# Windowed attention and an MLP-mixer in one kernel: the last batch's normalising in two tasks, one key copy on another engine, new ranks

## The chip, the cores and the metric

The kernel runs on one core of a Trainium2 chip. Inputs arrive in float32, the arithmetic on the matrix engine is in bfloat16, and the result is float32. The metric is the device time of one execution in microseconds. The engines are called by the names of the profile: PE is TensorE (matrix products), PEld its weight loads, DVE is VectorE, ACT is ScalarE, POOL is GpSimd and SP is SyncE, which issues DMAs.

## The reference

Four batches of eight heads, sequence 768, head size 64. Each query sees the 128 newest keys and the first four keys (the "sinks"). The eight heads' outputs side by side are the input x (768 x 512) of a mixer layer with a token product and a channel product.

```python
scores = (q @ k.T) / sqrt(64)              # per batch and head, 768 x 768
keep = (pos_k < 4) | ((pos_q - pos_k >= 0) & (pos_q - pos_k < 128))
a = exp(where(keep, scores, -1e9) - max)   # then a / sum(a)
x = concat_heads(a @ v)                    # 4 x 768 x 512
h = relu(x.T @ w_tok1) @ w_tok2            # 512 x 768
u = x + h.T
out = u + relu(u @ w_ch1) @ w_ch2          # w_ch1 512 x 1536, w_ch2 1536 x 512
```

## The kernel before

**The work.** The 32 pairs of batch and head are cut into eight groups of four heads, numbered g = 0 to 7; batch b holds the groups 2b and 2b + 1. Inside a group, j = 0 and 1 are its two pairs of heads. The rows of a group's key axis are six tiles of 128.

For each group the steps are, in the order of the data: load q and k in float32; cast to bfloat16 (`make_cast`); transpose on PE into a PSUM bank and copy the result to SBUF as `qT` and `kT` (`make_turn`; groups 5 to 7 transpose by DMA instead); copy eight sink columns of `kT` into `ks` (`make_ks`); score products on PE, where for groups 0 and 1 a product with `mneg` first puts the mask into PSUM, and `exp` on ACT into `pT` (`make_scores`); for groups 2 to 7 the mask is applied to `pT` afterwards by POOL or DVE; the product with v, six row tiles a group (`make_pv`). v carries a column of ones, so that each of the four heads has 64 sums and, as the 65th, its denominator. Normalising is a reciprocal of four denominators per row (`nc.vector.reciprocal`, 128 x 4) and a multiplication of 128 x 256 from PSUM into `x_b`.

After the two groups of a batch come the token products (`make_tok`) and the channel products (`make_channel`). Batches 1 to 3 make the second channel product from seven half-size products per pair of row tiles, with sums that DVE forms (`products`), and batch 3 some of the first too (`pairs_of_tiles`).

**The order.** No loop sets the order of the instructions. Every step is a `Task` with the engines that may run it, an estimated cost on each, the tasks it depends on, and a priority. `Plan.order` runs a list schedule over these: whenever an engine is free by the estimates, it takes the ready task of lowest priority number whose PSUM bank is free. A task that may run on several engines is taken by one only if it would end there no more than 0.12 us after the best. The instructions are then emitted in that planned order, so each engine runs its own fixed list, and real waits are semaphores. The priorities are overwritten from `RANK`, one number for each of 963 tasks in the order in which they are made.

**What the change touches.** `FIRST_TURNS` (line 19) names, for the four pairs of heads of groups 0 and 1, the engine of the PSUM-to-SBUF copy of q and of k. `SPLIT_TC` cuts these copies of group 0 into two halves of 384 columns. The entry of the second pair of heads reads `[('ACT', 'DVE'), 'ACT']`: its q copies may run on ACT or DVE, its two k copies run on ACT (line 439 in the profile, where a copy on DVE or POOL is line 441). `KS_ENG` (line 48) names the engines of the sink-column copies. In `make_pv`, groups 0 and 1 (`g < GB`, GB is 2) normalise in two tasks: the reciprocal on DVE (line 969) and the multiplication, on DVE (line 975) or, for group 1, also on ACT, where it would be four ACTIVATE instructions of 64 columns with the reciprocal as a per-row scale (line 978). Groups 2 to 7 have one task on DVE with both instructions (lines 962 and 963). For b of 2 or 3 this task also waits for the earlier readers of `x_b`, the list `old`.

Other names in the rows: `ps_sa`, `ps_sb` are the two double PSUM banks of the scores, `ps_ga` to `ps_gd` the four single banks; `rca` to `rcd` hold reciprocals; `vsink` is the sinks' part of v, made by DVE from `vs_b`; L1070 and L1068 are the relu on DVE and ACT, L1233 and L1143 the sums of the fast products, L1291 and its neighbours the reads of their results, and L484 issues loads.

Of the kernel before, what the change touches and what calls it, by code (L numbers as in the profile page):

```python
# [18 lines left out]
FIRST_TURNS = [[('ACT', 'DVE'), 'ACT'], [('ACT', 'DVE'), 'ACT'], ['DVE', 'DVE'], ['DVE', 'ACT']]  # L19
# [28 lines left out]
KS_ENG = {0: ('POOL', 'ACT', 'DVE'), 1: ('POOL', 'ACT', 'DVE'), 2: ('POOL',), 3: ('ACT',), 4: ('POOL', 'ACT', 'DVE'), 5: ('ACT', 'DVE'),  # L48
    6: ('ACT', 'DVE'), 7: ('ACT', 'DVE')}
# [7 lines left out]
RANK = [-500, 24, 27, 449, 556, 90, 80, 0, 0, 50, 50, 150, 100, 200, 150, 1557, 74, 556, 219, 901, 901, 1065, 1145, 1361, 1701, 2045,  # L57
    1972, 2310, 2575, 2855, 3040, -150, 210, 350, 300, 330, 1773, 1470, 1468, 1409, 1411, 1823, 3185, 3282, 100, 259, 239, 205, 529,
    441, 514, 701, 663, 12, 531, 585, 585, 803, 857, 904, 570, 625, 662, 836, 1004, 1070, 1212, 1232, 978, 783, 604, 682, 873, 890,
    1001, 1017, 1122, 1134, 1252, 1269, 1449, 1440, 1631, 1634, 1820, 1607, 1622, 1746, 1916, 1972, 2056, 2011, 2069, 2414, 2134, 2278,  # L60
    2211, 2076, 2192, 2225, 981, 1023, 1075, 1303, -80, 1101, 1155, 1359, 1497, 1218, 1243, 1456, 1658, 1757, 1741, 1402, 927, 1673,
    1786, 1330, 1627, 1802, 1987, 1822, 1997, 1906, 2226, 2157, 2089, 2268, 2285, 2171, 2215, 2218, 2278, 2338, 1814, 2488, 2447, 2471,
    2243, 2478, 2531, 2269, 2618, 2348, 2413, 2500, 2313, 2399, 2479, 2522, 2566, 2598, 2630, 2650, 3144, 2587, 2619, 2651, 2972, 3042,
    3021, 3102, 2824, 2894, 2923, 2683, 2775, 2825, 3070, 3151, 2874, 2924, 3720, 3190, 3624, 4010, 3559, 3645, 3364, 3450, 3169, 3360,
    4114, 4200, 3429, 3485, 3764, 3550, 3349, 3317, 3234, 3323, 3886, 3972, 3396, 3782, 4049, 4135, 4340, 4179, 4179, 4835, 4121, 3907,
    3984, 4070, 4405, 4508, 4320, 4556, 4657, 4846, 4722, 4889, 4592, 4682, 4940, 5048, 5243, 5329, 5308, 5394, 4787, 4965, 5380, 5489,
    5864, 5609, 5816, 6220, 6350, 6424, 6396, 6544, 6734, 6764, 6582, 6949, 7169, 7560, 7620, 7684, 7166, 7635, 7851, 7980, 8234, 8166,
    8276, 8556, 8685, 8750, 3803, 3379, 3879, 3250, 3951, 4009, 4307, 4313, 3662, 3717, 3629, 3747, 3921, 3905, 4244, 4328, 4418, 4535,
    4613, 4719, 5103, 5204, 5230, 5320, 4854, 5140, 4982, 4860, 5217, 5353, 4942, 5124, 5488, 5569, 5574, 5630, 5695, 5751, 5730, 5801,
    5765, 5851, 4780, 4997, 4738, 5070, 4877, 4961, 4843, 4898, 5313, 5300, 5346, 5361, 5516, 5536, 5542, 5595, 5686, 5800, 5924, 5993,  # L70
    5947, 6087, 6234, 5724, 5712, 5815, 6260, 7238, 6150, 6622, 6717, 6815, 6630, 7305, 6683, 6899, 6975, 7172, 7010, 7242, 7044, 7222,
    6008, 6035, 5283, 5969, 7257, 7374, 7252, 7428, 7592, 7694, 7859, 7548, 7634, 7734, 7721, 7808, 7984, 7764, 7867, 8129, 7971, 8042,
    8284, 7807, 7927, 8409, 3698, 4250, 4385, 4595, 4547, 4690, 4642, 4812, 9086, 8872, 8664, 8690, 8791, 8967, 9202, 9332, 8981, 9067,
    8916, 9004, 9157, 9223, 9332, 9418, 9267, 9369, 9866, 9972, 9625, 9711, 9560, 9706, 9610, 9776, 10427, 10513, 10232, 10318, 10167,
    10253, 10362, 10448, 10535, 10621, 10640, 10686, 10665, 10751, 10730, 10816, 10926, 11012, 10766, 11132, 10834, 11220, 10425, 10536,
    10678, 10788, 10740, 10835, 11039, 11720, 11205, 11274, 11355, 11480, 10297, 10383, 10795, 10883, 11417, 11528, 11548, 11634, 11613,
    11274, 11402, 11700, 11744, 11831, 11878, 11774, 10861, 10947, 10991, 11087, 11482, 11569, 12203, 12289, 11679, 12006, 12093, 12337,
    12398, 12485, 12532, 12411, 11205, 11322, 11810, 11896, 11875, 11962, 11941, 12027, 12072, 12911, 12997, 13614, 12107, 12224, 12271,
    12519, 5174, 4939, 5189, 5299, 5339, 5993, 5851, 5776, 5971, 6218, 6074, 6098, 6299, 6363, 6156, 6291, 6332, 6197, 6517, 6237, 6182,
    6915, 6565, 7443, 7491, 7560, 6838, 6967, 6993, 6898, 6900, 7014, 7606, 7773, 7637, 7275, 7959, 7992, 8253, 8302, 8014, 8102, 8084,  # L80
    8452, 8049, 8252, 8118, 8202, 5654, 5389, 5484, 5579, 5769, 5934, 5999, 6104, 7160, 6664, 6586, 6935, 7423, 6752, 7481, 8186, 8206,
    8363, 8446, 8536, 8729, 8747, 8816, 9046, 9237, 9146, 9263, 8583, 8643, 8779, 9007, 9270, 9349, 9125, 9158, 9397, 8842, 9421, 8892,
    9456, 9542, 9585, 9652, 9510, 9722, 8425, 7911, 7890, 8018, 9095, 9181, 9160, 9847, 9994, 10075, 10299, 9951, 10015, 10174, 10492,
    10556, 10564, 10037, 10135, 10519, 10080, 10194, 10769, 10124, 10254, 11249, 12716, 12802, 12271, 12357, 12544, 12550, 12529, 12615,
    12594, 12680, 12846, 12952, 12781, 12867, 13055, 13141, 13120, 13206, 13202, 13268, 13267, 13353, 13390, 13476, 13455, 13541, 13625,
    13711, 13965, 14051, 14200, 13986, 14030, 14116, 14205, 14327, 14490, 14576, 14903, 14989, 14360, 14446, 14783, 14849, 14968, 15054,
    15754, 15240, 14145, 14193, 14280, 14598, 14782, 15042, 15340, 15286, 15838, 15083, 15164, 15245, 14270, 14374, 14425, 14511, 15653,
    15739, 15544, 15630, 16404, 15294, 15512, 15902, 15979, 16065, 16298, 16248, 14555, 14646, 14632, 14729, 15913, 16171, 16130, 16228,
    16221, 16523, 16610, 16057, 16589, 16717, 16781, 16731, 14698, 14829, 15219, 15431, 16196, 16302, 16327, 16413, 16458, 16372, 16779,
    16544, 16654, 16750, 16831, 16618, 9034, 9129, 9224, 9414, 9649, 9604, 9699, 9984, 8297, 9726, 10044, 10347, 10981, 10894, 11119,  # L90
    12276, 12276, 12456, 12539, 12630, 12659, 12827, 12737, 13016, 13167, 13076, 13193, 12526, 12719, 12965, 12853, 13183, 12719, 13185,
    13253, 13332, 13377, 13356, 13417, 13520, 13576, 13545, 13546, 13590, 13676, 9949, 9794, 9319, 10424, 10079, 11024, 11374, 11469,
    9581, 10883, 11402, 12006, 12775, 11564, 12713, 13648, 13628, 13691, 13790, 13880, 13971, 14105, 14226, 14253, 14343, 14433, 13897,
    14009, 14247, 14485, 14646, 14829, 14621, 14699, 14828, 14873, 14852, 15223, 15033, 15090, 15068, 15140, 15107, 15333, 13835, 13921,
    13769, 13871, 15398, 15484, 15478, 15565, 15761, 16142, 15998, 15718, 15782, 15873, 15609, 15674, 15748, 15870, 15961, 16123, 16034,
    16108, 16348, 16087, 16168, 16473, 14326, 13779, 13832, 14241, 17053, 17124, 17195, 17266, 16720, 16806, 16785, 16871, 16850, 16936,
    16915, 17001, 16980, 17066, 17110, 17190, 17240, 17323, 17142, 17272, 17326, 17402, 17456, 17549, 17610, 17532, 17662, 17595, 17656,
    17735, 17795, 17045, 17153, 17175, 17261, 17305, 17091, 17370, 17428, 17435, 17502, 17467, 17500, 17553, 17865, 17872, 17781, 17842,
    17760, 17857, 17827, 17888, 17925, 17973, 17597, 17688, 17675, 17781, 17792, 17878, 17890, 17976, 18217, 18303, 18432, 18368, 18356,
    18442, 18421, 18507, 18077, 17525, 18200, 18316, 18496, 18621, 18702, 18723, 17971, 18029, 18173, 18268, 17955, 18363, 18020, 18430,  # L100
    18748, 18837, 18683, 18770, 18945, 18617, 18803, 19031, 18476, 19162, 19210, 19105, 18086, 18396, 18151, 18463, 18814, 18900, 18889,
    18966, 19141, 19010, 19097, 19228, 19338, 19425, 19473, 19302, 18526, 18609, 18552, 18689, 19207, 19293, 19272, 19359, 19403, 18737,
    19392, 19469, 19555, 19614, 17123, 19490, 19564, 19684, 19589, 19664, 19528, 19622, 19657]
STRASSEN = {1, 2, 3}
EARLY_P = {1: 0, 2: 0, 3: 4}
TURNS = '10 20 11 21 60 50 61 40 70 51 41 30 12 71 22 62 52 31 72 32 42'
S_CHUNK = 2
S_ENG = {1: ('DVE',), 2: ('DVE',), 3: ('DVE',)}
T_ENG = ('POOL', 'DVE')
HALF_PAIRS = 2  # L110
TILES = '05 0b 04 0a 03 p0 09 02 08 p1 15 1b 14 1a 13 19 12 18'

SEM = 0.05
# [214 lines left out]
def dve(n):  # L328
    return n * 0.00104 + 0.065
# [11 lines left out]
def kernel(  # L341
# [14 lines left out]
    B, H, S, D = q.shape  # L356
# [1161 lines left out]
```

## Time and profile before

| what | value |
|---|---|
| time, median of 13 runs | 199.39 us (198.97 to 200.59) |
| the profiled execution's own time | 200.41 us |
| its span, first to last instruction | 198.7 us |
| instructions | 4652 |
| granted TensorE clock | 1.00 throughout |
| DMA | 31.01 MB, mean 156 GB/s |

The profiled execution took 200.41 us, of which 1.7 us lie outside its span; it is 1.02 us above the median. A row of the windows view names a stretch and then the busy time of each engine in it, with the number of instructions in brackets. A row of the timeline gives start, duration, engine, source line, operation, tiles written and read, shapes, and, in square brackets, the idle time before it and what ended it. A PE row's duration contains the time in which the array waited in mid-instruction, so a PE that is busy for a whole stretch can still have lost time there.

### The profile page before, as it was taken

Reading aid. Unit: us, or ns where it says so; the run is one execution under the profiler, and the core shown is the slowest. Engines: PE = TensorE matmul, PEld = TensorE weight load, DVE = VectorE, ACT = ScalarE, POOL = GpSimd, SP = SyncE. Lnnn points to the kernel's source line nnn. Section 1 sums busy time; section 2 is a strip of 40 time slices with the busy share of each in tenths; the row PEclk is TensorE's granted clock in tenths of the full one; section 3 lists DMA queues with packets and bytes.
Section 4 is the critical chain, followed back from the end, with each engine's and each line's share of the span. In section 5 each row is a group of like instructions: output and inputs, shape, how many; then the busy total and the mean of one; then the engine's idle time right before and its main releaser. Section 6 shows DMA issues by size and latency. Waiting matters only on the chain.

```text
span 198.7 us, 4652 instructions
## 1 busy us (share of the span) xinstructions
PE 191.8 (97%) x1795; PEld 129.5 (65%) x1795; DVE 140.1 (71%) x321; ACT 107.3 (54%) x189; POOL 86.7 (44%) x151
## 2 busy tenths in 40 slices
PE   7899999999998999999999999999999999999993
PEld 2443876656675564665765787667687787567882
DVE  3688871587759677835558776367898979189973
ACT  2799378889898644177535301966843002765100
POOL 8984432125999763078770110891990000120000
PEclk9999999999999999999999999999999999999999
DMA  5999999999399979699999996250000157200044
GB/s 175 367 221 181 208 206 332 229 259 213 84 273 185 269 158 154 180 139 214 235 187 117 185 204 210 110 137 0 0 3 0 30 131 240 80 3 0 26 158 136
DMA packets 75016, 31.01 MB, mean 156 GB/s; under 512 B 63666, under 2 KB 71474, under 8 KB 74994
## 3 DMA queue, kind: packets, MB, share of 16 engines
q1 hardware_dynamic: 44082, 18.85, 42.4%
q0 software_dynamic: 29680, 10.22, 42.4%
q10 hardware_dynamic: 1232, 1.64, 2.3%
q8 instruction: 14, 0.23, 0.5%
q14 instruction: 8, 0.07, 0.1%
HBM read 26.77 MB, written 6.29 MB: 166 GB/s over the span
## 4 chain that ended last, share of the span: by engine, by line
PE 85%; ACT 4%; DVE 3%; DMA 3%; POOL 2%; issue 1%; POOLq 0%; DVEq 0%
PE ps_gd L1111 8%; PE ps_gb L1111 8%; PE ps_ga L1111 7%; PE ps_gd L1258 6%; PE ps_gb L1258 5%; PE ps_gc L1111 5%; PE ps_gc L1258 4%; PE ps_ga L1258 3%; DMA q32a<-in_q_dram 3%; PE ps_sa L1258 2%; PE ps_gb L1366 2%; PE ps_sa L830 2%; PE ps_sb L830 2%; PE ps_gd L1366 2%; PE ps_gd L1009 2%; PE ps_ga L1366 1%
## 5 line engine op out<-in xcount | busy, mean ns | idle before, releaser
L1111 PEld LDWEIGHTS <-w_ch 128*128 128x128 bf16 x352 | 33.3, 98 | 20.5 <-issue 0.6
L1258 PEld LDWEIGHTS <-v 128*128 128x128 bf16 x222 | 21.2, 98 | 4.2 <-issue 0.2
L1068 ACT ACTIVATE v<-ps_gb 128x384 bf16<-128x384 f32 x20 | 9.8, 490 | 17.9 <-PE ps_gb L1111 13.6
L1068 ACT ACTIVATE v<-ps_gc 128x384 bf16<-128x384 f32 x13 | 6.4, 489 | 16.2 <-PE ps_gc L1111 15.5
L1111 PE MATMUL ps_gd<-uTa,w_ch 128*128 128x384 bf16 x72 | 14.7, 326 | 0.0
L1068 ACT ACTIVATE v<-ps_gd 128x384 bf16<-128x384 f32 x19 | 9.3, 491 | 6.4 <-PE ps_gd L1111 6.2
L1068 ACT ACTIVATE v<-ps_ga 128x384 bf16<-128x384 f32 x16 | 7.8, 490 | 5.4 <-PE ps_ga L1111 5.3
L1366 PEld LDWEIGHTS <-v 128*128 128x128 bf16 x72 | 6.3, 97 | 6.8 <-issue 1.3
L1111 PE MATMUL ps_gb<-uTa,w_ch 128*128 128x384 bf16 x52 | 10.6, 326 | 0.0
L1009 PEld LDWEIGHTS <-w_tok 128*128 128x128 bf16 x96 | 9.2, 98 | 1.8 <-issue 0.2
L1111 PE MATMUL ps_gb<-uTb,w_ch 128*128 128x384 bf16 x48 | 9.8, 326 | 0.0
L441 POOL CAST of<-u_sbb 128x256 f32<-128x256 bf16 x1 | 0.7, 691 | 19.6 <-DVE vab L1143 19.6
L484 POOL DMA_DIRECT2D vaa<-in_v_dram x4 | 6.0, 1492 | 7.3 <-PE ps_gc L943 6.0
L1111 PE MATMUL ps_ga<-uTa,w_ch 128*128 128x384 bf16 x40 | 8.1, 326 | 0.0
L1111 PE MATMUL ps_ga<-uTb,w_ch 128*128 128x384 bf16 x40 | 8.1, 326 | 0.0
L484 POOL DMA_DIRECT2D vab<-in_v_dram x4 | 5.8, 1452 | 5.3 <-PE ps_gb L1033 2.4
L885 POOL TENSOR_TENSOR pTa<-pTa,mask 128x512 bf16<-128x512 bf16 x2 | 2.3, 1153 | 13.1 <-ACT pTa L874 13.1
L874 ACT ACTIVATE pTc<-ps_sb 128x768 bf16<-128x768 f32 (+1 forms) x6 | 5.5, 924 | 3.6 <-PE ps_sb L830 3.6
L441 DVE CAST kba<-k32a 128x768 bf16<-128x768 f32 x4 | 4.1, 1046 | 4.6 <-DMA k32a<-in_k_dram 4.6
L441 POOL CAST qbb<-q32b 128x768 bf16<-128x768 f32 x5 | 4.1, 820 | 7.1 <-DMA q32b<-in_q_dram 7.1
L441 POOL CAST kbb<-k32b 128x768 bf16<-128x768 f32 x5 | 4.5, 893 | 5.8 <-DMA k32b<-in_k_dram 5.8
L830 PEld LDWEIGHTS <-kTa 64*128 64x128 bf16 x96 | 3.5, 94 | 4.8 <-issue 3.8
(453 smaller groups left out, 593.9 us busy)
## 6 DMA issues: line engine op xcount, KB each, us to landing
q32a<-in_q_dram SPq DMA_DIRECT2D x4, 384.0 KB, 4.6
vaa<-in_v_dram POOLq DMA_DIRECT2D x4, 384.0 KB, 11.2
vab<-in_v_dram POOLq DMA_DIRECT2D x4, 384.0 KB, 11.3
w_ch<-in_moe_w_ch_dram POOLq DMA_DIRECT2D x3, 512.0 KB, 15.2
w_ch<-in_moe_w_ch_dram POOLq DMA_DIRECT2D x2, 768.0 KB, 19.8
q32b<-in_q_dram SPq DMA_DIRECT2D x8, 192.0 KB, 4.6
k32b<-in_k_dram SPq DMA_DIRECT2D x8, 192.0 KB, 5.7
out_dram<-oa SPq DMA_DIRECT2D x4, 256.0 KB, 7.0
```

What stands on the lines that cost most here:

```text
L441: on(t).tensor_copy(out=o, in_=i)
L484: t = add(eng, hold, lambda t: e.dma_start(out=o, in_=i), deps, prio=prio, dma=work, run=run)
L830: nc.tensor.matmul(half(slot, i)[:, at:at + w].rearrange("p (c q) -> p c q", q=P), qkT(kT, g, j)[ds(64 * i, 64), kt], qkT(qT, g, j)[ds(64 ...
L874: nc.scalar.activation(dst[:, :, 512 * u:512 * u + w], ps_s[slot.at[1]][:, :, 0:w], AF.Exp, scale=scale)
L885: on(t).tensor_tensor(out=dst[:, :, 0:2 * P], in0=dst[:, :, 0:2 * P], in1=mask0.rearrange("p i c q -> p i (c q)"), op=ALU.mult)
L1009: nc.tensor.matmul(flat(slot)[:, 0:GH * D], w_tok1[:, n, ts(tt, P)], x[:, n, ds(a * GH * D, GH * D)], start=(n == 0), stop=(n == NT - 1))
L1068: nc.scalar.activation(o, i, AF.Relu)
L1111: nc.tensor.matmul(flat(slot)[:, 0:HS], w_ch1[:, c, ts(ft, P)], uT_[:, c, ds(half * HS, HS)], start=(c == 0), stop=(c == NC - 1))
L1258: nc.tensor.matmul(flat(slot)[:, 0:cw], A[n][0][:, x, ts(i, P)], W[n][:, x, ds(c0, cw)], start=(first and x == 0), stop=(x == NH - 1), ski ...
L1366: nc.tensor.matmul(flat(slot)[:, 0:cw], v1[:, ft, ts(st, P)], w_ch2[:, ft, ds(c0, cw)], start=(ft == 0), stop=(ft == NF - 1 and (b > 0 or ...
```

## The change

Three switches and the table of ranks. The second pair of heads' key copy in group 0 goes to DVE. The sink-column copies may run on other sets of engines in four groups. The groups 6 and 7, which are the last batch, normalise in two tasks as the groups 0 and 1 do, so that their multiplication may run on DVE or ACT; it keeps the wait for `old`, the reciprocal does not have it. As each of 12 tasks becomes two, `RANK` has 975 entries instead of 963. Of the older entries 211 change by more than 15, up to 1200, and 18 by 15 or less; the rest keep their value.

```diff
-FIRST_TURNS = [[('ACT', 'DVE'), 'ACT'], [('ACT', 'DVE'), 'ACT'], ['DVE', 'DVE'], ['DVE', 'ACT']]
+FIRST_TURNS = [[('ACT', 'DVE'), 'ACT'], [('ACT', 'DVE'), 'DVE'], ['DVE', 'DVE'], ['DVE', 'ACT']]
...
-KS_ENG = {0: ('POOL', 'ACT', 'DVE'), 1: ('POOL', 'ACT', 'DVE'), 2: ('POOL',), 3: ('ACT',), 4: ('POOL', 'ACT', 'DVE'), 5: ('ACT', 'DVE'),
-    6: ('ACT', 'DVE'), 7: ('ACT', 'DVE')}
+KS_ENG = {0: ('ACT', 'DVE'), 1: ('POOL', 'ACT', 'DVE'), 2: ('POOL', 'ACT', 'DVE'), 3: ('ACT', 'DVE'), 4: ('POOL', 'ACT', 'DVE'), 5:
+    ('ACT', 'DVE'), 6: ('ACT', 'DVE'), 7: ('ACT', 'DVE')}
...
-RANK = [-500, 24, 27, 449, 556, 90, 80, 0, 0, 50, 50, 150, 100, 200, 150, 1557, 74, 556, 219, 901, 901, 1065, 1145, 1361, 1701, 2045,
...
+RANK = [-500, 24, 37, 449, 556, 90, 80, 0, 0, 50, 50, 150, 100, 200, 150, 1517, 74, 556, 219, 901, 901, 1065, 1145, 1361, 1701, 2045,
...
+NORM_ACT = {6, 7}
...
-            if g < GB:
+            old = [*mixers[b - 2].add, *mixers[b - 2].tok1, *mixers[b - 2].s_use[2]] if b >= 2 else []
+            if g < GB or g in NORM_ACT:
                 def er(t, slot=slot, r=r):
                     nc.vector.reciprocal(r, flat(slot)[:, 0:GH * D1].rearrange("p (h d) -> p h d", h=GH)[:, :, D:D1])
...
                 m = add("DVE", 0.1, er, [m, last_rc], prio=pr(g, "no"))
-                G.norm.append(add(("ACT", "DVE") if g else "DVE", {"ACT": 0.8, "DVE": dve(GH * D)}, e, [m], prio=pr(g, "no"),
+                G.norm.append(add(("ACT", "DVE") if g else "DVE", {"ACT": 0.8, "DVE": dve(GH * D)}, e, [m, *old], prio=pr(g, "no"),
                                   slot=slot, frees=True))
                 rc_use[slot_rc] = G.norm[-1]
                 continue
-            old = [*mixers[b - 2].add, *mixers[b - 2].tok1, *mixers[b - 2].s_use[2]] if b >= 2 else []
             G.norm.append(add("DVE", dve(4) + dve(256) + 0.1, e, [m, *old, last_rc], prio=pr(g, "no"), slot=slot, frees=True))
```

Ranks that the prediction speaks of, by the task they belong to (before, then after; unchanged where one number stands):

| task | rank |
|---|---|
| group 0, second pair: q copies, two halves | 857, 904 |
| group 0, second pair: k copies, two halves | 1004, 1070 |
| group 1, first pair: cast of q, cast of k | 981 to 1011, 1023 to 1053 |
| group 0: sink-column copies | 1212; 1232 to 592 |
| group 0: v product of row tiles 1 and 2 | 1607 to 1307, 1916 to 1316 |
| group 1, row tile 0: v product | 2089 to 2699 |
| group 4, first pair: exp of the first and second of its units | 6915 to 6695, 6565 to 6535 |
| group 6: normalising of six row tiles | 13253 ... 13676 to pairs 12885, 12909 ... 13338, 13383 |
| group 7: normalising of six row tiles | 14699 ... 15333 to pairs 15084, 15265 ... 15487, 15532 |

## The prediction

> **What bounds the kernel now.** I read the page first, then the windows of 5 us, then the PE's own waits, and last the timelines of ACT and DVE in the stretches where PE loses time.
>
> ```profile
> PE 191.8 (97%) x1795; PEld 129.5 (65%) x1795; DVE 140.1 (71%) x321; ACT 107.3 (54%) x189; POOL 86.7 (44%) x151
> ```
>
> PE is busy for 97% of the span, and in the channel products it is at its pace: groups of four matmuls of 384 columns start every 0.65 us in the chain of waits, 163 ns each. So a change that leaves the products alone can only win back what PE loses to waits. The PE waits view names, in 8 to 24 us and in 56 to 66 us:
>
> ```profile
> PE ps_sb L813 <- ACT pTc L874: 0.4, 1, 0.4
> PE ps_sa L817 <- ACT pTa L874: 0.2, 1, 0.2
> ...
> PE ps_gb L837 <- DVE h1b L1070: 0.4, 1, 0.4
> PE ps_ga L1366 <- DVE kTa L441: 0.4, 1, 0.4
> PE ps_gb L751 <- DVE kba L441: 0.2, 1, 0.2
> ```
>
> That is 0.6 us of waits for `exp` in front and 1.0 us for DVE in the middle. A busy PE hides more. From the starts of its rows less the columns at the pace above, and less the 0.09 us that every change between score products and full-height products costs, I get 1.3 us in 8 to 24 us (0.18 at 8.2, 0.23 at 10.0, 0.18 at 16.9, 0.43 at 18.0, 0.24 at 21.8), 1.4 us in 60 to 64.3, and 0.3 us in 146 to 152. The start (0.6 us for the first cast) and the last 3.3 us (reads and stores after PE's end at 195.4) aren't touched by a switch.
>
> In front the bound is ACT, with DVE close behind. The windows of 8:15, 15:22, 58:65 and 150:156:
>
> ```profile
> 8.00:15.00 7.00, 6.74 (x77) 3.50 (x73) 5.32 (x9) 6.95 (x13) 6.34 (x9) 1.00 1.62 255
> 15.00:22.00 7.00, 6.51 (x90) 3.29 (x87) 5.50 (x16) 6.53 (x9) 3.28 (x7) 1.00 1.73 189
> 58.00:65.00 7.00, 6.08 (x63) 4.16 (x61) 5.71 (x7) 5.68 (x9) 6.91 (x12) 1.00 1.67 221
> 150.00:156.00 6.00, 6.00 (x68) 4.89 (x67) 5.58 (x16) 2.03 (x5) 0.00 (x0) 1.00 0.00 0
> ```
>
> ACT has 6.95 of 7 us (fourth busy figure), DVE 5.32. The timelines of the two engines there:
>
> ```profile
> 10.17 0.53 ACT L439 ACTIVATE kTa<-ps_gd 128x384 bf16<-128x384 bf16 x1
> 10.54 0.86 ACT L874 ACTIVATE pTa<-ps_sb 128x768 bf16<-128x768 f32 x1
> 11.23 0.55 ACT L439 ACTIVATE kTa<-ps_gd 128x384 bf16<-128x384 bf16 x1
> 11.60 1.10 ACT L874 ACTIVATE pTb<-ps_sa 128x1024 bf16<-128x1024 f32 x1
> 14.83 0.83 ACT L874 ACTIVATE pTc<-ps_sb 128x768 bf16<-128x768 f32 x1
> ...
> 9.30 1.02 DVE L441 COPY qTa<-ps_gc 128x384 bf16<-128x384 bf16 x2 [1.07 <-PE ps_gc L751]
> 10.24 0.55 DVE L441 CAST qbb<-q32b 128x768 bf16<-128x768 f32 x1
> 10.70 0.74 DVE L441 CAST kbb<-k32b 128x768 bf16<-128x768 f32 x1
> 12.96 0.96 DVE L441 COPY kTb<-ps_ga 128x768 bf16<-128x768 bf16 x1 [0.24 <-PE ps_ga L751]
> ```
>
> The reader should see that the two key copies stand between `exp` instructions on ACT, and that the moved copies would stand on DVE in front of the casts from which the next group's scores come.
>
> For the normalising, DVE's timelines at 151 and at 23.6 us:
>
> ```profile
> 151.36 0.17 DVE L962 RECIPROCAL rcc<-ps_gb 128x4 f32<-128x4 f32 x1
> 151.56 0.42 DVE L963 TENSOR_TENSOR x_bb<-ps_gb,rcc 128x256 bf16<-128x256 f32 x1
> 151.91 0.17 DVE L962 RECIPROCAL rcd<-ps_gd 128x4 f32<-128x4 f32 x1
> ...
> 23.62 0.17 DVE L969 RECIPROCAL rcc<-ps_ga 128x4 f32<-128x4 f32 x1
> 23.71 0.15 DVE L969 RECIPROCAL rcd<-ps_gc 128x4 f32<-128x4 f32 x1
> ```
>
> In one task each multiplication starts 0.20 us after its reciprocal and a pair takes 0.55 us. In two tasks the reciprocals overlap, 0.09 us apart.
>
> **What the Trainium skill says.** "ScalarE: Activation LUTs", section "What ACT_TABLE_LOAD costs", prices an ACTIVATE at 186 ns + 0.833 ns a column, 93 ns more for each per-row operand, and lets neighbours overlap by 93 ns. 384 columns give 506 ns; the trace has 486 to 552, so it agrees. "TensorE: Matmul & The Clock Gate", section "Back-to-back issue gap", has N / 2.4 + 2.5 ns for a warm matmul, 162.5 ns at 384 columns, against 163 here. "SBUF — State Buffer", section "Who interferes with whom", says that a cast on DVE and an instruction of GpSimd can lock each other out for a whole instruction. The trace fits: the cast of `kba` at 61.01 us took 2.39 us beside a row of POOL masks, where the one at 10.24 took 0.55.
>
> **The change part by part.**
>
> *Key copies to DVE.* ACT loses two ACTIVATEs. The next starts 0.37 us after each (10.17 to 10.54, 11.23 to 11.60), so ACT is freed of 0.74 us in a stretch in which it is never idle. DVE gains two copies of 0.47 us (half of the 9.30 row's 1.02, less overlap), 0.94 us. By their ranks, 1004 and 1070 against 1011 and 1053 for the casts, one half comes before the casts and one after. DVE's holes up to 12.96 sum to little: 0.24 us before `kTb`. Its cast of q may go to POOL, which is a choice the planner had before (0.46 us less on DVE; POOL has 6.34 of 7 us in use, and behind a cast there would queue the issues of the weight loads). The chain ends in the `exp` of group 1 at 14.83: ACT was held until then by its own work, while `kTb` ended at 13.92 and the shortest way from there (score products 0.3 us, and their turn) reaches ACT at about 14.4. So of the 0.74 us the first 0.4 are free of DVE, if DVE's chain doesn't move; if it moves by the whole 0.94 the `exp` starts at 15.3. The bounds are 0.74 us won and 0.5 lost. I take 0.5 won: the masks' products on PE can go ahead, and the three copies of group 1 behind `kTb` have slack, since DVE's casts of `vs_b` at 15.28 (2.0 us in four) can be put off until `vsink` at 18.07. A cap comes from PE: it can't give back more than the 1.3 us that it lost there, and the 0.43 at 18.0 and 0.18 at 16.9 are direct waits for `exp`.
>
> *Earlier v products of group 0* (ranks down by 300 and 600). Row tile 2 needs `vsink`, which ends at 19.4, so no rank brings it ahead of 19.46; nothing. Their normalising is on DVE, off the path until 24.0.
>
> *Sink-column engines.* Group 0 used DVE (0.45) and ACT (0.20) already, so losing POOL changes nothing. In group 2 POOL waited 6.86 us idle before its two copies, with nothing behind them; in group 3 ACT's pair took 0.44. Nothing for both; if DVE is chosen, 0.45 us each beside other work. PE is full there until 60 us.
>
> *Normalising in two tasks.* No instruction is added while the multiplication stays on DVE, and the reciprocal needs no wait for `old`. By the rows above, a tile falls from 0.55 to about 0.42 (23.62 to 24.88 holds three), so 12 tiles free at most 1.5 us of DVE, which is 93% busy in 150:156. On ACT, L978 has no row. By the skill's price it would be 4 x (186 + 93 + 53) less three overlaps of 93, about 1.05 us as an estimate, beside an ACT that has 2.03 of 6 us. PE lost 0.3 us here, so the gain is 0 to 0.3. Against it, group 7's ranks rise by some 100 to 570, so that fast-product sums (L1233) come before it; the bank stays held, and the token products behind it wait: up to 0.5 us lost. I take 0.2 won.
>
> *The ranks elsewhere.* They move the middle, where 1.0 to 1.4 us are lost to DVE's casts of `q32a` and `k32a`: one waits for a load that lands at 59.46, the other for POOL. Neither cause is removed. The two ranks of group 4's `exp` let ACT follow at once. Bounds: 0.9 us won, if DVE and POOL happen to miss each other, to 0.6 lost, one more cast such as that of 2.39. I take 0.2 won. The long blocks of equal shifts (by 30 between 79 and 106 us) keep the order among themselves.
>
> Sum: 0.5 + 0.2 + 0.2 = 0.9 us. Against the profiled execution 200.41 gives 199.5; it is 1.02 above the median, so for the median 199.39 - 0.9 = 198.5 us.
>
> **Rivals.**
> - *DVE becomes the bound in front* (slower). The 0.94 us move group 1's chain whole, no cast goes to POOL, and ACT idles before 15.3. For: only 0.24 us of holes. Against: the chain's slack and the choice of POOL. It decides once DVE's casts and copies move by more than about 0.45 us; the full move costs 0.5, and with 0.2 to 0.3 us in later waits of PE for `exp` the time is 200.1.
> - *The middle gets worse* (slower): another cast meets POOL's masks, 0.6 us and nothing won in front: 200.0.
> - *Hidden*: PE's lost time in front is mostly its own turnarounds, and what ACT frees is spent waiting for DVE; 199.3.
> - *The middle closes*: both casts miss POOL, 0.9 on top of the forecast: 197.6.
>
> **Numbers.** Forecast 0.50 (its own range 198.0 to 198.8), middle closes 0.08, hidden 0.16, DVE bound 0.18, middle worse 0.08. Faster by over 0.3% (about what can be told from no change) is 0.58, within it 0.16, slower 0.26. The range 197.6 to 200.1 takes in the bounds of the middle and of the front's loss.
>
> **What would show it.** `kTa<-ps_gd` on DVE and no ACT idle between 10 and 21 us; the first token product (24.00 in the chain) at 23.5; the PE wait for `pTc` gone. For the rival: `pTc` at 15.2 or later behind an idle ACT. In 130 to 156 us, reciprocals in clusters, and L978 on ACT or none; a PE wait for `x_bb` there would say that the new ranks cost. A sum of PE waits in 60 to 64 us above 1.4 would make the prediction wrong.

## The result and the profile after

The changed kernel takes 200.5 us (median of 11 executions, 200.28 to 201.75) against 199.36 us for the kernel before in the same comparison (48 executions). The ratio is 1.0058 with a 95% interval of 1.004 to 1.0076: 0.58% slower. Beside the experiments the kernel before was run again, with medians of 199.1 to 199.33 us. Each ratio below is against it in the same comparison; it leaves out the few executions in a slower state, most of them over 203 us, and need not equal the quotient of two medians. The profiled execution of the changed kernel took 200.65 us, with a span of 198.9 us.

In the changed kernel's lines the numbers are two higher than before: L443 is the copy or cast on VectorE (441 before), L753 a transpose, L832 a score product, L941 and L945 a product with v, L981 the multiplication on ACT. In the experiments they differ again, since the table of ranks takes fewer lines there. First the page's busy times and the windows that were shown of before.

```profile
PE 192.6 (97%) x1795; PEld 130.0 (65%) x1795; DVE 140.6 (71%) x323; ACT 108.8 (55%) x196; POOL 85.1 (43%) x148
```
```profile
8.00:15.00 7.00, 6.16 (x64) 2.92 (x63) 5.74 (x10) 5.68 (x9) 6.80 (x8) 1.00 1.62 255
15.00:22.00 7.00, 6.64 (x78) 3.20 (x78) 6.10 (x16) 6.60 (x9) 3.51 (x9) 1.00 1.71 188
58.00:65.00 7.00, 6.93 (x81) 4.76 (x77) 5.45 (x11) 6.70 (x10) 6.35 (x11) 1.00 1.45 238
150.00:156.00 6.00, 6.00 (x65) 4.82 (x62) 5.73 (x16) 2.97 (x9) 0.00 (x0) 1.00 0.01 3
```

In 8 to 15 us ACT fell from 6.95 busy microseconds to 5.68, as the change intends, but PE did less too: 64 matmuls started there instead of 77. In 58 to 65 us PE does more than in the profile before. PE's own waits over the whole span:

```profile
PE ps_ga L1475 <- DVE warm L447: 1.2, 1, 1.2
PE ps_ga L753 <- DVE kbb L443: 0.6, 1, 0.6
PE ps_sa L819 <- ACT pTc L876: 0.4, 1, 0.4
PE ps_sa L819 <- ACT pTa L876: 0.2, 1, 0.2
```

The second line is new: PE waits 0.6 us for the cast of `kbb`. VectorE's timeline shows why the cast is late, and ACT's shows what the prediction had named as the sign of its slower rival.

```profile
10.72 1.01 DVE L443 COPY kTa<-ps_gd 128x384 bf16<-128x384 bf16 x2
11.65 0.86 DVE L443 CAST qbb<-q32b 128x768 bf16<-128x768 f32 x1
12.44 1.17 DVE L443 CAST kbb<-k32b 128x768 bf16<-128x768 f32 x1
13.53 0.94 DVE L443 COPY qTb<-ps_gb 128x768 bf16<-128x768 bf16 x1
```
```profile
15.04 0.38 ACT L863 ACTIVATE pka<-ps_gc 128x256 bf16<-128x256 f32 x1 [1.24 <-PE ps_gc L839]
...
16.75 0.81 ACT L876 ACTIVATE pTc<-ps_sb 128x768 bf16<-128x768 f32 x1
```

The two key copies stand ahead of the casts. ACT was idle for 1.24 us before 15.04, works without a pause from there, and `pTc` comes at 16.75. It looks as if VectorE had become the bound. The experiments show that this reading is wrong. PE's timeline of the same stretch holds the line that matters:

```profile
14.92 0.51 PE L753 MATMUL ps_gd<-ident,qbb 128*128 128x128 bf16 x6
15.27 0.19 PE L941 MATMUL ps_gb<-vaa,pTa 128*128 128x65 bf16 x1
...
15.52 0.50 PE L753 MATMUL ps_gc<-ident,kbb 128*128 128x128 bf16 x6
15.85 0.49 PE L819 MATMUL ps_sb<-mneg,ident 128*128 128x384 bf16 x2
16.27 0.34 PE L832 MATMUL ps_sb<-qTb,kTb 64*128 64x256 bf16 x4
```

The product with v of row tile 1 of group 0 now stands ahead of group 1's transposes and first scores. Before, it stood behind them.

To compare executions I use the times at which PE starts certain pieces of work, in us from the start of the span:

| execution | group 1's first scores | first channel product, batch 0 | first token product, batch 1 | first scores of group 4 | first channel product, batch 3 | PE's end | span |
|---|---|---|---|---|---|---|---|
| before, as profiled for the prediction | 14.45 | 30.51 | 58.43 | 65.28 | 166.52 | 195.40 | 198.68 |
| before, profiled again | 14.60 | 30.55 | 58.47 | 63.98 | 165.23 | 194.11 | 197.39 |
| after | 16.27 | 31.53 | 59.55 | 65.20 | 166.47 | 195.35 | 198.94 |
| copies only | 15.00 | 30.93 | 58.85 | 64.37 | 165.61 | 194.49 | 197.77 |
| after, copies back | 16.22 | 31.49 | 59.50 | 65.02 | 166.18 | 195.06 | 198.63 |
| after, front back | 14.47 | 30.55 | 58.57 | 64.08 | 165.24 | 194.12 | 197.68 |
| before, v ranks only | 14.46 | 31.77 | 59.69 | 65.21 | 166.45 | 195.34 | 198.62 |
| after, six memsets | 16.33 | 31.59 | 59.61 | 65.13 | 166.29 | 195.17 | 198.45 |
| same, row tile 1 later | 15.04 | 30.67 | 58.69 | 64.20 | 165.36 | 194.24 | 197.51 |
| same, and copies back | 15.45 | 30.73 | 58.75 | 64.73 | 165.89 | 194.78 | 198.07 |

The changed kernel loses 1.0 us before 31 us, keeps that loss to the end, and its span ends 0.3 us later after PE's end than that of the kernel before.

### The profile page after: what moved, and what is told of

Read it like the earlier page. It is cut to its first block, busy times and chain, and to the rows that moved or that the text cites. A ratio compares the mean times of both kernels' runs of the same rounds, so it can differ in the third digit from the quotient of the medians.

```text
span 198.9 us, 4647 instructions
## 1 busy us (share of the span) xinstructions
PE 192.6 (97%) x1795; PEld 130.0 (65%) x1795; DVE 140.6 (71%) x323; ACT 108.8 (55%) x196; POOL 85.1 (43%) x148
## 3 DMA queue, kind: packets, MB, share of 16 engines
q10 hardware_dynamic: 1232, 1.64, 2.3%
## 4 chain that ended last, share of the span: by engine, by line
PE 84%; DMA 5%; ACT 4%; DVE 3%; issue 1%; SPq 0%; DVEq 0%; ACTq 0%
PE ps_gb L1113 8%; PE ps_gd L1113 7%; PE ps_ga L1113 7%; DMA k32a<-in_k_dram 5%; PE ps_gd L1260 5%; PE ps_gb L1260 5%; PE ps_gc L1113 4%; PE ps_gc L1260 4%; PE ps_ga L1260 3%; PE ps_gd L1368 3%; PE ps_gc L1368 3%; PE ps_sa L1260 3%; PE ps_sa L832 2%; PE ps_sb L832 2%; PE ps_sb L1113 2%; PE ps_gd L1011 2%
## 5 line engine op out<-in xcount | busy, mean ns | idle before, releaser
L1070 ACT ACTIVATE v<-ps_gb 128x384 bf16<-128x384 f32 x18 | 8.9, 492 | 13.0 <-PE ps_gb L1113 13.0
L1197 POOL TENSOR_SCALAR v<-q32b 128x384 bf16<-128x384 f32 x1 | 1.2, 1176 | 27.6 <-DVE q32b L1183 27.6
L1113 PE MATMUL ps_gd<-uTa,w_ch 128*128 128x384 bf16 x56 | 11.4, 326 | 0.0
L1113 PE MATMUL ps_gb<-uTa,w_ch 128*128 128x384 bf16 x56 | 11.4, 326 | 0.0
L1070 ACT ACTIVATE v<-ps_ga 128x384 bf16<-128x384 f32 x18 | 8.8, 490 | 4.7 <-PE ps_ga L1113 4.6
L1070 ACT ACTIVATE v<-ps_gd 128x384 bf16<-128x384 f32 x15 | 7.4, 491 | 5.4 <-PE ps_gd L1113 5.1
L1072 DVE TENSOR_SCALAR v<-ps_gd 128x384 bf16<-128x384 f32 x7 | 3.9, 557 | 7.6 <-PE ps_gd L1113 7.6
L1113 PE MATMUL ps_ga<-uTa,w_ch 128*128 128x384 bf16 x44 | 8.9, 326 | 0.0
L443 POOL CAST kbb<-k32b 128x768 bf16<-128x768 f32 x5 | 4.9, 984 | 5.9 <-DMA k32b<-in_k_dram 5.9
L876 ACT ACTIVATE pTb<-ps_sa 128x1024 bf16<-128x1024 f32 (+1 forms) x7 | 6.9, 990 | 0.5 <-PE ps_sa L832 0.5
L906 POOL TENSOR_SCALAR_AFFINE_SELECT pTc<-pTc 128x256 bf16<-128x256 bf16 (+1 forms) x12 | 6.2, 517 | 1.5 <-ACT pTc L876 1.5
```

Of the source, the lines that this page charges most:

```text
L443: on(t).tensor_copy(out=o, in_=i)
L876: nc.scalar.activation(dst[:, :, 512 * u:512 * u + w], ps_s[slot.at[1]][:, :, 0:w], AF.Exp, scale=scale)
L906: nc.gpsimd.affine_select(out=cur, in_=cur, compare_op=ALU.is_ge, fill=0.0, base=0, pattern=[[0, hi - lo], [1, P]], channel_multiplier=-1)
L1070: nc.scalar.activation(o, i, AF.Relu)
L1072: nc.vector.tensor_scalar(out=o, in0=i, scalar1=0.0, scalar2=None, op0=ALU.max)
L1113: nc.tensor.matmul(flat(slot)[:, 0:HS], w_ch1[:, c, ts(ft, P)], uT_[:, c, ds(half * HS, HS)], start=(c == 0), stop=(c == NC - 1))
```

## The experiments

### The kernel before, once more

No edit.

> The kernel before, unchanged, for a second profile. The profiled execution of before took 200.41 us, 1.05 above the median 199.36, and its PE lost 1.4 us in 60 to 64 us. If that loss belongs to the odd execution, a look at about 199.2 us shows under 0.5 us lost there and the PE chain some 1 us earlier from 66 us on, with the same front (first token product at 24.0). If the loss is always there and the difference lies outside the span, the span is again near 198.7 and the loss is 1.4.

It took 199.21 us, ratio 1.0007 (0.9982 to 1.0032), and its profile has no loss in the middle. VectorE's timeline there:

```profile
59.36 0.74 DVE L441 CAST qba<-q32a 128x768 bf16<-128x768 f32 x1 [1.12 <-DMA q32a<-in_q_dram]
60.02 0.41 DVE L1070 TENSOR_SCALAR h1b<-ps_gb 128x256 bf16<-128x256 f32 x1
60.48 0.78 DVE L441 CAST kba<-k32a 128x768 bf16<-128x768 f32 x1
```

The same two casts took 1.26 and 2.39 us in the execution that the prediction was read from. So its 1.3 us between 60 and 64 us were that execution's own. To judge by the times most executions don't have them: of 37 of the kernel before in a later comparison, seven took 200.2 to 200.7 us and 30 under 199.9. The rows of the table above are compared with this second profile.

### The copies alone

The kernel before with its planned order; only the engine of the two key copies is set afterwards.

```diff
         todo = plan.order()
+        for t in Gs[0].T[1][1]:
+            t.on = 'DVE'
```

> Before's order of all tasks, only the two key copies of the second pair of heads run on DVE instead of ACT, at the places that the plan of before gives them: the first half ahead of the two casts of group 1, the second half behind them. Theory (the copies themselves make DVE the bound in front): the cast of k for group 1 ends 0.4 to 0.5 us later, the PE transposes of it wait, the first token product starts 0.4 to 0.9 us later, time 199.8 to 200.2. Rival (the ranks, not the copies, cost the time): ACT is freed of 0.7 us, the token product is not later, time 199.0 to 199.5.

It took 199.55 us (22 executions), ratio 1.0016 (1.0003 to 1.0029). PE runs 0.4 us behind the kernel before from 12.6 us on and never catches up. In before's order the copies on VectorE cost about 0.4 us on PE in this profile and about 0.2 us in the medians, and what ACT gains by them isn't used.

### The changed kernel with the copies back on ACT

The same edit of the changed kernel, with `'ACT'`.

> After's order of all tasks, only the two key copies back on ACT, where it had 1.24 us idle at 13.8. Theory (copies on DVE ahead of the casts are the cause): casts of group 1 start 0.9 us sooner, the PE wait for the cast of k (0.6 us) is gone, token product 0.5 to 0.9 us sooner, time 199.6 to 200.0 against 200.5. Rival (the ranks of the front, which put the sinks' exp ahead of the third exp and row tile 1 ahead of scores): the wait of ACT stays, 200.3 to 200.6.

It took 200.49 us, ratio 1.0055 (1.0035 to 1.0076): nothing came back. PE's waits in 8 to 24 us:

```profile
PE ps_gb L941 <- DMA vaa<-in_v_dram: 0.5, 1, 0.5
PE ps_sa L819 <- ACT pTc L876: 0.4, 1, 0.4
...
```

With the copies on ACT the wait for `kbb` is gone, and PE waits at row tile 1's product instead, for a transfer: that of v. Group 1's scores still start at 16.2.

### The normalising alone

The kernel before with `NORM_ACT = {6, 7}`; each of the twelve tasks becomes two with the old rank r and r + 1. The rest is as before.

> Before, with only the normalising of groups 6 and 7 in two tasks; each reciprocal has the rank of the old task and its multiplication that rank plus one; front and middle are in the order of before. Theory (the split is neutral, since PE has 0.3 us to win there at most): 199.2 to 199.6. Rival (the split and its move to ACT cost, as the 0.4 us that after falls back between 133 and 147 us suggest): 199.7 to 200.0.

It took 201.1 us, ratio 1.009 (1.0055 to 1.0125). PE's waits in 140 to 156 us, and VectorE's timeline there:

```profile
PE ps_sb L1213 <- DVE x_ba L1188: 0.5, 1, 0.5
PE ps_gd L1213 <- DVE v L1025: 0.3, 1, 0.3
PE ps_gb L964 <- DVE x_bb L931: 0.3, 1, 0.3
```
```profile
144.08 1.53 DVE L1188 TENSOR_TENSOR k32a<-q32a,v 128x768 bf16<-128x768 bf16 x1
...
152.09 0.17 DVE L925 RECIPROCAL rcc<-ps_ga 128x4 f32<-128x4 f32 x1
152.19 0.53 DVE L1188 TENSOR_TENSOR x_ba<-v 128x768 bf16<-128x768 bf16 x1
152.63 0.42 DVE L931 TENSOR_TENSOR x_bb<-ps_ga,rcc 128x256 bf16<-128x256 f32 x1
```

A sum now stands between a reciprocal and its multiplication, and PE waits for `x_bb`. Another sum took 1.53 us at 144.08, where the one at 151.62 took 0.56; it lay over GpSimd's product with the mask, 1.15 us from 144.04. From the first channel product of batch 2 to that of batch 3 it takes 45.4 us, against 43.8 in both profiles of the kernel before. The split with the old ranks is a loss. The profiled execution took 202.04, above the median, and also holds the stall in the middle (6.79 us from the first token product of batch 1 to group 4's first scores).

### The front put back

The changed kernel with the copies on ACT, `KS_ENG[0]` and all ranks of steps planned before 38 us as before. The order of the four engines up to there is then that of the kernel before, and the later order is the changed kernel's.

> The changed kernel with its first 38 us put back: the key copies on ScalarE, the sink-column engines of group 0 and the ranks of all steps planned before 38 us as before (the planned order of the four engines up to there is that of the kernel before); everything later is the changed kernel's. Theory (about 1.0 us of the loss lies in front of 30 us and 0.3 in the tail after the last store): the first channel product starts at 30.5 instead of 31.5 us, and the time is about 199.5 us, ratio 1.000 to 1.002. Rival 1 (the late ranks and the two-task normalising are what costs, the front is made up for later): 200.2 or more. Rival 2 (the later ranks are a real gain that the front hides): below 199.0, ratio under 0.998.

It took 199.71 us (7 executions, 199.38 to 200.35), ratio 1.0035 (1.0019 to 1.0051), a little above what was expected. Its profile gives the reason for 0.3 us, the tail (below). Up to there it lies on the kernel before: first channel product 30.55, PE's end 194.12 against 194.11. So the changed ranks after 38 us and the two-task normalising with its new ranks win nothing and lose nothing on PE in this pair of profiles; the remainder of the median isn't explained.

### The ranks of the v products alone

The kernel before with nine ranks changed: those of the v products of row tiles 1, 2 and 3 and of the normalising of row tiles 0, 1 and 2.

```diff
-... 1634, 1820, 1607, 1622, 1746, 1916, 1972, 2056, 2011 ...
+... 1374, 1520, 1307, 1922, 1146, 1316, 1372, 1456, 1711 ...
```

> The kernel before with nothing but the ranks of group 0's v products of row tiles 0 to 3 and of their normalising as changed; the key copies stay on ScalarE. In the planned order the v product of row tile 1 comes ahead of group 1's first scores. Theory (the ranks' order costs by itself, since that product waits for an exp and TensorE's order is fixed): group 1's first scores move from 14.6 to 15.3 us or later with a wait of TensorE of 0.4 to 0.7 us in front of the product of row tile 1 near 14.4 us, and the time is 0.4 to 1.0 us longer, ratio 1.002 to 1.005. Rival (the order is free, and the loss of the changed kernel in front comes only from the copies on VectorE): the scores stay within 0.15 us and the ratio within 0.999 to 1.001.

It took 200.31 us (4 executions), ratio 1.0063 (1.0049 to 1.0076): as much as the whole loss, with both key copies on ACT. PE's waits in 8 to 30 us, then PE's timeline:

```profile
PE ps_gd L963 <- DVE x_ba L929: 0.7, 1, 0.7
PE ps_sb L767 <- ACT pTc L828: 0.5, 1, 0.5
PE ps_gb L893 <- DMA vaa<-in_v_dram: 0.5, 1, 0.5
...
```
```profile
14.46 0.34 PE L784 MATMUL ps_sb<-qTb,kTb 64*128 64x256 bf16 x4
15.30 0.19 PE L893 MATMUL ps_gb<-vaa,pTa 128*128 128x65 bf16 x1 [0.50 <-DMA vaa<-in_v_dram]
...
16.39 0.51 PE L705 MATMUL ps_ga<-ident,kbb 128*128 128x128 bf16 x6
```

My expectation had the cause half wrong. The wait isn't for an `exp` but for v, and group 1's first scores go ahead of it and don't move; what is held is all that follows. Of the 1.2 us by which the first channel product is late, this wait is one part. The other is a second wait, for the normalised `x_ba`, 0.7 us in front of the token product at 27.07, which the same nine ranks brought about.

### The tail

First the kernel before with three GpSimd instructions given to the engines that have them in the changed kernel, then the changed kernel with six memsets added.

```diff
         todo = plan.order()
+        plan.tasks[266].on, plan.tasks[267].on, plan.tasks[954].on = 'DVE', 'ACT', 'ACT'
```

> The kernel before in its own planned order, with three GpSimd instructions given to the engines that have them in the changed kernel: the two sink-column copies of group 2 (to VectorE and ScalarE) and one late read of a result (to ScalarE). Theory (the 0.30 us between the last store and the end of the span go with the length of GpSimd's instruction stream, not with the work): TensorE ends within 0.15 us of the kernel before, the clear of the semaphores at the end starts about 0.3 us after GpSimd's previous instruction instead of 0.03 us, and the time is about 0.3 us longer, ratio 1.0015. Rival (the tail depends on something else in the changed kernel): 0.03 us as before, ratio 1.000.

```diff
                 idle(N_IDLE)
+        for _ in range(6):
+            nc.gpsimd.memset(scratch[:, 0:1], 0.0)
```

> The changed kernel with six more memsets of one column on GpSimd, after all its work, where it is idle; it then has as many GpSimd instructions as the kernel before. Theory (as above): the clear of the semaphores starts 0.03 us after the previous instruction again, and the time falls by 0.3 us from 200.5 to 200.2 us. Rival (the tail has another cause): 0.33 us as in the changed kernel, time 200.5 us.

The first took 199.39 us, ratio 1.002 (1.0008 to 1.0033), where the kernel before had 199.1; PE's end stayed at 194.12. The second took 200.17 us (4 executions), where the changed kernel had 200.5. GpSimd's last records, start and duration in us:

```
                          DRAIN            RANGE_CLEAR      gap    GpSimd's records
before, again             196.82 + 0.10    196.95 + 0.14    0.03   206
before, three off         196.82 + 0.09    197.23 + 0.14    0.32   200
after                     198.06 + 0.10    198.50 + 0.14    0.33   200
after, six memsets        197.88 + 0.10    198.01 + 0.14    0.03   206
```

The gap is that between the end of GpSimd's previous record and the clear of the semaphores, with which every execution ends. In the four profiles with 200 records it is 0.32 or 0.33 us, in the ten with 205 to 208 it is 0.03, and both kernels are in both groups. So 0.3 us of the loss have nothing to do with the work: they come with the moved sink-column copies and one late read. What in the shorter stream makes the clear wait stays open.

### Row tile 1 put back, with and without the copies

The changed kernel with the six memsets; group 0's v product of row tile 1 and its normalising are moved in the lists to where row tile 0's are.

```diff
         todo = plan.order()
+        late = plan.tasks[85:88]
+        todo = [x for x in todo if x not in late]
+        todo[todo.index(plan.tasks[82]):todo.index(plan.tasks[82])] = late[:1]
+        todo[todo.index(plan.tasks[83]):todo.index(plan.tasks[83])] = late[1:]
```

> The changed kernel with the six memsets of the run above (so that the tail is the short one), and with one step moved back in TensorE's list: group 0's v product of row tile 1 comes directly ahead of that of row tile 0, as before, instead of ahead of the second transposes of group 1; its normalising moves along on VectorE. The key copies stay on VectorE. Theory (TensorE stood at row tile 1 until v had landed near 15.2 us, with all of group 1 queued behind it, and that hid what the copies cost): no wait for v, group 1's first scores at 15.0 us or earlier instead of 16.3, the first channel product at 30.9 instead of 31.6 us, and 199.6 us, 0.6 less than the 200.17 of the changed kernel with the memsets; the 0.4 that remain in front are the copies'. Rival 1 (the copies on VectorE hold the chain in this order as well): 200.1 us and the first channel product at 31.5. Rival 2 (the copies are free once v no longer holds TensorE): 199.2 us.

It took 199.45 us (14 executions, 199.03 to 199.93), ratio 0.9999 (0.998 to 1.0019); by the medians 0.25 us are left (199.45 against 199.20). One product, moved by about 1 us in PE's list with its normalising, takes away 0.9 us (first channel product 30.67 instead of 31.59), with the copies on VectorE. First the wait and PE's timeline of the changed kernel with the six memsets, then PE's timeline with row tile 1 moved.

```profile
PE ps_gb L941 <- DMA vaa<-in_v_dram: 1.1, 1, 1.1
```
```profile
13.73 0.51 PE L753 MATMUL ps_gd<-ident,qbb 128*128 128x128 bf16 x6
15.31 0.20 PE L941 MATMUL ps_gb<-vaa,pTa 128*128 128x65 bf16 x1 [1.08 <-DMA vaa<-in_v_dram]
...
15.57 0.50 PE L753 MATMUL ps_gc<-ident,kbb 128*128 128x128 bf16 x6
...
16.33 0.34 PE L832 MATMUL ps_sb<-qTb,kTb 64*128 64x256 bf16 x4
```
```profile
13.73 0.51 PE L753 MATMUL ps_gd<-ident,qbb 128*128 128x128 bf16 x6
14.29 0.50 PE L753 MATMUL ps_gc<-ident,kbb 128*128 128x128 bf16 x6
14.62 0.49 PE L819 MATMUL ps_sb<-mneg,ident 128*128 128x384 bf16 x2
15.04 0.34 PE L832 MATMUL ps_sb<-qTb,kTb 64*128 64x256 bf16 x4
...
16.18 0.20 PE L941 MATMUL ps_gb<-vaa,pTa 128*128 128x65 bf16 x1
```

Up to 13.73 both run alike. Then one stands still until v is there, with group 1's transposes and scores, which need no v, behind it; the other does these first and finds v landed. Compare the first of the two with the changed kernel's own profile above. There PE came 1.2 us later to the transposes ahead of row tile 1 (14.92 instead of 13.73): VectorE's copy of `qTa` started 0.45 us later, and its casts took 0.86 and 1.17 us instead of 0.55 and 0.74. Yet row tile 1 started at nearly the same time, 15.27 instead of 15.31. In that execution PE came to it just as v landed, so the trace shows the wait for the cast of `kbb` and none for v.

> As the run before, with the two key copies on ScalarE. Theory: the first channel product at 30.6 us and 199.2 us, the level of the kernel before; 0.4 less than with the copies on VectorE, as in the pair of before and copies only. Rival (another part of the new front order costs too, such as the earlier exp of the sink scores or the earlier mask unit): 199.6 us or more.

It took 199.53 us, ratio 1.0002 (0.9985 to 1.002), not the 199.2 expected. With the copies on ACT the first channel product comes at 30.73, with the copies on VectorE at 30.67. So no cost of the copies on VectorE is seen in the changed kernel's order, and the 0.4 us that they cost alone belong to before's order. On this point the second rival of the run before was right, and my theory wrong. This run's own rival, that another part of the new front order costs too, isn't excluded: with the copies on ACT the first channel product comes 0.2 us later than in the kernel before.

### The load behind v

Only GpSimd's issue of the load of `w_tok1` moves, from directly behind v's to behind that of group 1's v.

```diff
         todo = plan.order()
+        late = plan.tasks[18]
+        todo.remove(late)
+        todo.insert(todo.index(plan.tasks[17]) + 1, late)
```

> The changed kernel with the six memsets and with nothing moved but one issue of a load: that of w_tok1, which GpSimd issues at 3.2 us behind the load of group 0's v, goes behind the load of group 1's v (near 7.9 us). TensorE's, ScalarE's and VectorE's lists are those of the changed kernel. Theory (v's landing near 15.2 us is what TensorE stands at, and it lands late because it shares its queue with the load issued right after it): v lands 0.5 to 2 us earlier, TensorE's wait before row tile 1 shrinks by as much or goes, group 1's first scores start at 15.9 us or earlier instead of 16.3, and the time is 199.6 to 199.9 us instead of 200.17. Rival 1 (v lands no earlier, since the loads of q and k bound it): 200.2 us, with the same wait. Rival 2 (v lands earlier but the wait is replaced, for instance by one for group 1's v or for w_tok1 near 24 us): a wait of TensorE there, and 200.2 us or more.

It took 200.26 us, ratio 1.005 (1.0035 to 1.0065). v landed 13.9 us after its issue instead of 13.7, and PE waited as before:

```profile
PE ps_gb L941 <- DMA vaa<-in_v_dram: 1.2, 1, 1.2
```

The load behind it doesn't make v late. What does stays open: in the view of transfers the 16 DMA engines are busy for 90% or more of every slice from about 3 to 18 us, so v shares them with other loads, but no way of bringing v earlier other than this was tried.

### One task for the normalising again

The kernel with row tile 1 moved back, with `NORM_ACT = set()`; each of the twelve tasks has the rank of its reciprocal.

> The run with row tile 1 moved back and the copies on VectorE (199.45 us there), with the normalising of groups 6 and 7 in one task again; each of the twelve tasks has the rank that its reciprocal has in the changed kernel, the other ranks stay. Theory (two tasks with refitted ranks are worth nothing that can be measured; the 1.6 us that they lost in 143 to 154 us with the old ranks came from ranks that let sums go first): 199.3 to 199.6 us, and from the first channel product of batch 2 to that of batch 3 43.8 to 43.9 us as in both kernels. Rival 1 (two tasks win what the prediction took, 0.2 us): 199.6 to 199.9 us. Rival 2 (they cost even with refitted ranks): below 199.2 us.

It took 199.58 us (199.18 to 200.26), ratio 1.0003 (0.9975 to 1.0031). In the profile the stretch between the first channel products of batches 2 and 3 takes 44.2 us instead of 43.9, with a wait of 0.3 us for `x_bb`. In the medians the difference is 0.1 us, inside the scatter. So with ranks made for two tasks, two tasks are 0 to 0.3 us better than one.

## Why the prediction was wrong

- **Earlier v products of group 0 ("nothing").** This step failed, and it decided the result. I looked at row tile 2, which needs `vsink`, and not at row tile 1, which doesn't and whose rank falls by 300 as well. Its product needs v, and v's landing stood in the profile before. The view of transfers, for 0 to 18 us (bytes, then us from issue to landing), and GpSimd's timeline:

```profile
vaa<-in_v_dram POOLq DMA_DIRECT2D x1, 384.0 KB, 13.7
```
```profile
1.55 1.66 POOL L484 DMA_DIRECT2D vaa<-in_v_dram  x1
```

  Issued at 1.55, v is there at about 15.25; before, PE first read it at 15.9. The row's own end, 3.2 us, is no landing. The Trainium skill says so in "Perfetto Trace Analysis", section "DMA Instruction — SWDGE (GPSIMD)": the profiler's end is when the descriptors have been generated, not when the data have moved. Here the two lie 12 us apart. That a product which waits holds what is behind it is also in the skill: "PSUM — Partial Sum Buffer", section "Engine vs sequencer instructions", has matmuls start and complete in program order. The runs agree: in the run with six memsets the transposes behind row tile 1 begin at 15.57, where they begin at 14.29 with it out of the way. The price of the step is 0.9 us (first channel product 31.59 against 30.67), where the prediction had 0.
- **Key copies to DVE ("I take 0.5 won").** Alone they lose 0.4 us on PE, inside the stated bounds of 0.74 won and 0.5 lost and near the bad end. In the changed order, with row tile 1 out of the way, no cost is seen: the first channel product starts at 30.67 with them on VectorE and at 30.73 with them on ACT. The order that the prediction read from the ranks, one half before the casts and one after, didn't come about either: both halves come before them. ACT did get free time, as said. The first token product then starts at 23.05 with the copies on VectorE and at 23.45 with them on ACT, and the last at 26.27 and 26.69. But then PE waited 0.2 us for a relu on ACT. In the last run, in which PE has the same order up to there, that wait is missing and the first channel product comes at 30.32, 0.2 us ahead of the kernel before. So single profiles show up to 0.4 us won by the copies in front, and the medians (199.45, 199.53 and 199.58 us) don't show it.
- **Ranks elsewhere ("0.2 won").** Nothing. Most executions of the kernel before don't have the 1.0 to 1.4 us in the middle, so the 0.2 us were taken off a median that has no such loss. From the first token product of batch 1 to group 4's first scores it takes 5.5 us in the second profile of the kernel before and in six of the eight rows below it in the table, with either set of ranks, and 6.85 in the first. The Trainium skill's statement on casts beside GpSimd, which the prediction drew on ("SBUF — State Buffer", section "Who interferes with whom"), fits, and the traces show which instruction of GpSimd it was here. `kba`'s cast of 2.39 us, from 61.01 on, lay over this product with the mask:

```profile
61.84 1.14 POOL L885 TENSOR_TENSOR pTd<-pTd,mask 128x512 bf16<-128x512 bf16 x1
```

  In the normalising alone it lay over the same product and took 2.19 us. In the twelve other profiles the cast ended before that product began and took 0.54 to 0.91 us; in the second profile of the kernel before it took 0.78, with only shorter masks beside it. This stall came and went between executions of the same kernel; whether ranks could keep the two apart wasn't tried.
- **Normalising in two tasks ("0.2 won", bounds 0.3 won and 0.5 lost).** No gain is seen against the kernel before: from the first channel product of batch 2 to that of batch 3 it takes 43.8 us there and 43.9 in the changed kernel. What the prediction built on, that a tile falls from 0.55 to about 0.42 us on VectorE, didn't come about. The reciprocals don't cluster in the changed kernel, and a tile takes as long as in one task:

```profile
150.17 0.18 DVE L972 RECIPROCAL rcb<-ps_sa 128x4 f32<-128x4 f32 x1
150.38 0.42 DVE L978 TENSOR_TENSOR x_bb<-ps_sa,rcb 128x256 bf16<-128x256 f32 x1
150.73 0.17 DVE L972 RECIPROCAL rcc<-ps_gd 128x4 f32<-128x4 f32 x1
```

  With old ranks the split loses far more than the bound of 0.5, 1.8 us in the medians. Ten of the twelve multiplications stayed on VectorE. Of the two on ACT one row:

```profile
151.77 0.93 ACT L981 ACTIVATE x_bb<-ps_sa,rcd 128x64 bf16<-128x64 f32 x4
```

  Four took 0.93 us, where the prediction's estimate was 1.05.
- **Sink-column engines ("nothing for both").** The sets of engines change in three groups, 0, 2 and 3, not in four. Nothing for the work, as said, but together with one late read that left GpSimd they bring 0.3 us at the end of the program, for which the prediction had no term.
- **The rival "DVE becomes the bound in front".** It had the right place and sign, and its sign in the profile came true (`pTc` at 16.75, after ACT had been idle). Its cause didn't: taking the copies off VectorE gives nothing back, and leaving them there while row tile 1 moves gives the 0.9 us back. Two causes had one sign, and the prediction gave no view that would have told them apart.

The time lies 2.0 us above the forecast of 198.5 and 0.4 above the range. The sum of what was found: 0.9 us for row tile 1 and 0.3 us for the tail make 1.2 us, against 1.14 us between the medians.

## What to carry to other kernels

Where an engine runs a fixed list, a step that is moved ahead must be checked for everything that it reads, transfers included: take the issue plus the time to landing from the view of transfers, and compare it with the time at which the step would come. If it would stand, all behind it on that engine stands, and what is freed on another engine may buy nothing, as here. And a loss that one profiled execution shows is only worth a gain if a second execution shows it too, above all where that execution is slower than the median.

## What was unexpected of the hardware

The clear of the semaphores at the end starts 0.03 us after GpSimd's previous record with 205 to 208 records on GpSimd and about 0.32 us after it with 200. Six memsets of one column that do nothing made the changed kernel 0.3 us shorter; three instructions taken off GpSimd made the kernel before 0.3 us longer, with the same work elsewhere and PE's end unchanged.
